# Five early slots, last routing tiles between them, and 1024-wide weight splits in a chain of attention and two expert layers

## The chip, the cores and the metric

The kernel runs on one core of one Trainium2 chip. The metric is device time in microseconds (us) for one execution of the whole program, as the median of three runs.

## What is computed

Three layers follow one another, with 4608 tokens of 512 values. The first is attention over keys and values that are pooled in groups of eight (8 batches, 8 heads, 576 queries, 72 pooled keys). The second is a gated product of two dense layers. The third sends each token to the one of eight experts that its logits choose. Cut to what matters:

```python
k_p = k.reshape(B, H, Sp, 8, D).mean(axis=3)          # v_p alike
attn = softmax(scale * q @ k_p.T)                     # 576 x 72 per head
x = (attn @ v_p), heads side by side                  # 4608 x 512
x = (x @ w_a * (x @ w_b)) @ w_out                     # 512 -> 1536 -> 512
logits = x @ w_gate                                   # 4608 x 8
e = argmax(logits); gate = softmax(logits)[e]
out = gate * (relu(x @ w1[e]) @ w2[e])                # 512 -> 1024 -> 512
```

## The kernel before

The engines are TensorE (PE, matmuls), VectorE (DVE), ScalarE (ACT), GpSimd (POOL) and SyncE (SP, which issues most DMAs). Each engine works through its own queue in order. Every f32 operand of a large matmul is split into a high part (a cast on ACT) and a low part (a subtraction, mostly on DVE), and each product is three matmuls: high x high, high x low, low x high. The order of instructions on each engine is laid out by a planner of the framework, from program order, priorities (`tc.high_priority()`) and its own model of durations. `tc.issue_after(ins)` forces the instructions of its block that run on the same engine as `ins` to stand behind `ins`.

**Start.** `half(b, j)` (L482) does the attention of one batch in two parts of 256 and 320 queries, in tiles of up to 128 queries. For each tile `softmax` (L404) makes scores on PE, their extremes on DVE (`mx`), 16 exponent steps on ACT (`pt`) and the division. For batch 0 `softmax` also builds `tails` on POOL, and `turned` (L523) transposes the probabilities on PE into `tp` and splits them into `th` and `tl`; the other batches go through DRAM instead (`send`, `receive`). Then `av` (L555) multiplies with the values. Meanwhile `convert(f)` (L620) splits the twelve pieces of the second layer's weights with ACT and DVE, `chain` forcing the first pieces behind steps of batch 0's softmax, and each stored piece releases the load of a later one (`load_raw`). `first` (L690) runs the second layer on batch 0 as its weights come in.

**Middle.** `moe1(s)` (L728) runs the second layer on tokens 512 at a time, nine times, with the attention of a later batch and the routing of an earlier result between its steps. `finish` copies four result tiles of 128 tokens (`x1s`) and makes a `route` generator for each (L640). Its first stage, up to `yield t`, computes the eight logits of a tile with eight products on DVE (L645), the winner and the exponents. Its second stage ranks the tokens with two small matmuls (`rk`, L670 and L671) and writes them with an indirect DMA from POOL into `rows` (L684), a DRAM table with one region per expert.

**Slots.** The third layer runs in slots of 256 tokens (`big`) or 128 (`small`) of one expert. A `Slot` (L190) has `load` (eight pieces of its expert's weights: DMA to `wr`, then the two parts into `w`), `fetch` (a gather of its tokens from `rows` by SP), `transpose` (L231 on DVE, then the split into `x`), `mm1` (96 matmuls of 256 columns for a big one, with `hidden` splitting each 512 columns of the relu into `hh` on ACT and `hl` on DVE), and `mm2` (48 matmuls of 512 columns for a big one, then `y` on ACT and an indirect DMA from POOL to the output). The weight tiles `w` rotate through 12 buffers, one and a half slots.

The first `NEARLY` = 4 slots are early: `early_table` fills their expert and position after the eighth of the nine steps, from the tokens known by then. The other 14 big slots and 5 small ones (some more under a condition at the end) come from `slot_table` (L906), which needs every token's rank. In the trace names end in `e` for early slots, `b` for big and `s` for small ones: `hle` is `hl` of an early slot, `gxb` the gathered rows of a later big one.

The order around the end of the middle part stands by hand, here from L886 on. The first stages of the last four routing tiles come ahead of all slots:

```python
for g in routes:
    while next(g) is None:
        pass
...
slots[1].load(0, 1, 2, 3)
slots[0].mm1()
slots[1].transpose()
...
slots[1].mm1()
with tc.issue_after(slots[1].last):
    step(routes, 99)
```

Then, in phase two (L1004), the table, and a loop over the slots that loads and transposes the next slot's input around each slot's `mm1` (L1022) and `mm2`. In the stage of the early slots the output tiles `y` come from the same pool as `x1s` (`p_x1`, L850). The weight buffers of phase two are a pool of its own (`p_wr`, 8 buffers), placed where the memory of the middle part was.

## Time and profile before

| what | value |
|---|---|
| median of 3 runs | 1544.84 us (1542.69 to 1544.87) |
| the profiled execution | 1544.62 us |
| its span, first to last instruction | 1542.8 us |
| PE busy | 1469.5 us, 95% |
| DVE, ACT, POOL busy | 984.4, 727.8, 313.3 us |
| mean granted clock of PE | 0.982 |

The profile's page gives the busy share of each engine in forty slices of the span, tenths of a slice as digits. Further views are tables of the same by chosen windows, lists of what each engine waited for, a timeline of instructions, groups of instructions by line, and the chain of waits that ended last. A matmul's duration overlaps with the next one's, so that the distance of two starts is the cost of one.

### The profile page before, as it was taken

How to read it: one execution, taken by the hardware profiler on the slowest of the kernel's cores; microseconds unless marked ns; L12 is line 12 of the kernel's file. 1: busy time of each engine (PE TensorE's matmuls, PEld its weight loads, DVE VectorE, ACT ScalarE, POOL GpSimd, SP SyncE). 2: the span in 40 equal slices, each digit the busy share in tenths (PEclk: the TensorE clock that was granted, in tenths of full speed). 3: DMA queues.
4: the chain of work that ended last, by engine and by line, in shares of the span. 5: the costliest groups of instructions: out<-in, count | busy, mean ns of one | idle time of the engine just before them, and what ended most of it. 6: DMA issues, size and time to landing. Idle time of an engine off the chain costs nothing.

```text
span 1542.8 us, 23808 instructions
## 1 busy us (share of the span) xinstructions
PE 1469.5 (95%) x7848; PEld 1255.5 (81%) x7848; DVE 984.4 (64%) x2446; ACT 727.8 (47%) x1878; POOL 313.3 (20%) x393
## 2 busy tenths in 40 slices
PE   4599899999999999999999999998989999999997
PEld 3499788888888888888888888887878898998986
DVE  8958594584664864845942727638867675757560
ACT  7858443534433433433432113234367665757561
POOL 2110112112111110210210000121233343433341
PEclk8799999999999999999999999999999999999998
DMA  8658644436435445344333224426289996969740
GB/s 308 207 195 290 202 150 129 154 117 178 137 113 164 130 127 167 116 132 151 122 123 99 76 82 164 157 76 191 102 274 319 301 297 213 289 217 294 237 144 28
DMA packets 145389, 268.97 MB, mean 174 GB/s; under 512 B 27049, under 2 KB 81065, under 8 KB 145264
## 3 DMA queue, kind: packets, MB, share of 16 engines
q1 hardware_dynamic: 139104, 247.44, 50.8%
q0 software_dynamic: 6160, 19.99, 3.3%
q8 instruction: 63, 1.03, 0.3%
q14 instruction: 62, 0.51, 0.1%
HBM read 223.45 MB, written 44.16 MB: 173 GB/s over the span
## 4 chain that ended last, share of the span: by engine, by line
PE 80%; DMA 7%; DVE 4%; ACT 4%; issue 3%; SPq 1%; POOL 1%; POOLq 0%; DVEq 0%; ACTq 0%
PE ab L754 11%; PE ab L755 11%; PE ab L756 11%; PE po L740 6%; PE po L741 6%; PE po L742 6%; PE hpb L273 3%; PE hpb L275 3%; PE hpb L274 3%; PE ypb L295 3%; PE ypb L296 3%; PE ypb L297 3%; PE sc L411 2%; PE av L555 2%; DMA wre<-in_w 1%
## 5 line engine op out<-in xcount | busy, mean ns | idle before, releaser
L755 PE MATMUL ab<-x,wab 128*128 128x512 f32 x768 | 302.3, 394 | 2.6 <-DVE x L187 2.6
L754 PE MATMUL ab<-x,wab 128*128 128x512 f32 x768 | 300.5, 394 | 0.2 <-ACT a L760 0.2
L756 PE MATMUL ab<-x,wab 128*128 128x512 f32 x768 | 300.5, 392 | 0.0
L645 DVE CUSTOM_DVE_ANT_0 junk<-x1s,wg 128x512 bf16<-128x512 f32 x288 | 205.4, 713 | 17.7 <-ACT x1s L781 11.6
L755 PEld LDWEIGHTS ab<-x,wab 128*128 128x128 f32 x768 | 144.2, 188 | 32.1 <-DVE x L187 2.8
L754 PEld LDWEIGHTS ab<-x,wab 128*128 128x128 f32 x768 | 144.2, 188 | 30.8 <-issue 1.0
L756 PEld LDWEIGHTS ab<-x,wab 128*128 128x128 f32 x768 | 144.3, 188 | 28.6 <-issue 0.2
L740 PE MATMUL po<-wo,gh 128*128 128x512 f32 x384 | 151.4, 394 | 0.0
L741 PE MATMUL po<-wo,gh 128*128 128x512 f32 x384 | 151.1, 394 | 0.0
L209 DVE TENSOR_TENSOR wb<-wrb,wb 128x512 fp32r<-128x512 f32 x168 | 126.2, 802 | 37.5 <-ACT wb L208 37.5
L742 PE MATMUL po<-wo,gl 128*128 128x512 f32 x384 | 143.5, 391 | 0.0
L208 ACT CAST wb<-wrb 128x512 fp32r<-128x512 f32 x224 | 126.0, 621 | 34.9 <-DMA wrb<-in_w 16.2
L186 ACT CAST gh<-a 128x512 fp32r<-128x512 f32 (+1 forms) x120 | 69.9, 584 | 137.1 <-DVE a L765 131.0
L760 ACT COPY a<-ab 128x512 f32<-128x512 f32 x96 | 56.8, 592 | 160.2 <-PE ab L756 123.3
L765 DVE TENSOR_TENSOR a<-ab,a 128x512 f32<-128x512 f32 x96 | 66.0, 687 | 96.9 <-PE ab L756 85.8
L684 POOL DMA_INDIRECT rows<-x1s,posu x36 | 39.0, 1083 | 434.7 <-DVE posu L683 176.9
L273 PE MATMUL hpb<-xb,wb 128*128 128x256 f32 x448 | 127.1, 284 | 0.0
L274 PE MATMUL hpb<-xb,wb 128*128 128x256 f32 x448 | 126.6, 283 | 0.0
L275 PE MATMUL hpb<-xb,wb 128*128 128x256 f32 x448 | 126.6, 283 | 0.0
L419 ACT ACTIVATE pt<-sc,mx 128x72 f32<-128x72 f32 (+1 forms) x320 | 98.5, 327 | 54.4 <-DVE mx L416 41.8
L447 POOL TENSOR_TENSOR pq<-pt,sm 128x256 f32<-128x256 f32 (+1 forms) x70 | 48.6, 713 | 341.5 <-DVE sm L425 208.5
L209 POOL TENSOR_TENSOR wb<-wrb,wb 128x512 fp32r<-128x512 f32 x56 | 76.9, 1394 | 91.5 <-ACT wb L208 90.5
(263 smaller groups left out, 3332.4 us busy)
## 6 DMA issues: line engine op xcount, KB each, us to landing
wrb<-in_w SPq DMA_DIRECT2D x112, 512.0 KB
wo<-wos SPq DMA_DIRECT2D x96, 512.0 KB
wrs<-in_w SPq DMA_DIRECT2D x40, 512.0 KB
wre<-in_w SPq DMA_DIRECT2D x32, 512.0 KB
vr<-in_v SPq DMA_DIRECT2D x48, 256.0 KB
raw<-in_wab SPq DMA_DIRECT2D x24, 512.0 KB
turns<-pq SPq DMA_DIRECT2D x28, 384.0 KB
gp<-turns SPq DMA_DIRECT2D x112, 96.0 KB
```

The source lines that it names most:

```text
L208: nc.scalar.copy(w[:, 0, hs], raw[:, hs])
L209: (nc.gpsimd if i%4==3 else nc.vector).tensor_tensor(out=w[:, 1, hs], in0=raw[:, hs], in1=w[:, 0, hs].bitcast(F32), op=ALU.subtract)
L273: nc.tensor.matmul(hp[:, fi], lhsT=wh, rhs=self.x[:, 0, k], start=k == 0, stop=False)
L274: nc.tensor.matmul(hp[:, fi], lhsT=wh, rhs=self.x[:, 1, k], start=False, stop=False)
L275: i = nc.tensor.matmul(hp[:, fi], lhsT=wl, rhs=self.x[:, 0, k], start=False, stop=k == NK - 1)
L645: nc.vector.tensor_tensor_reduce(out=junk, in0=x1s[:, :DM], in1=wg[:, e, :], scale=1.0, scalar=0.0, op0=ALU.mult, op1=ALU.add, accum_out=l ...
L740: nc.tensor.matmul(po[t], lhsT=gh[:, ts_], rhs=w[:, 0], start=f == 0, stop=False)
L741: nc.tensor.matmul(po[t], lhsT=gh[:, ts_], rhs=w[:, 1], start=False, stop=False)
L742: nc.tensor.matmul(po[t], lhsT=gl[:, ts_], rhs=w[:, 0], start=False, stop=f == NF1 - 1)
L754: nc.tensor.matmul(o, lhsT=wh, rhs=xh, start=k == 0, stop=False)
L755: nc.tensor.matmul(o, lhsT=wh, rhs=xl, start=False, stop=False)
L756: nc.tensor.matmul(o, lhsT=wl, rhs=xh, start=False, stop=k == NK - 1)
```

## The change

- `NEARLY` goes from 4 to 5, so there are 5 early slots and 13 later big ones; the three small tiles of each turn of `early_table` share a buffer.
- In `Slot.load` each piece of 1024 columns is cast by one instruction on ACT and subtracted by one on DVE, instead of two of 512 each with the subtraction on POOL for pieces 3 and 7.
- `hidden` keeps its DVE instruction as `self.hid`.
- For batch 0 the building of `tails` moves from `softmax` into `turned`, and a tile's `turned` is called after the next tile's `softmax`.
- The output tiles of the early stage get a pool of their own, `p_y`, with two buffers.
- The first stages of the four last routing tiles (`rate`) are called one by one after `slots[0].mm1()`, `slots[0].mm2()`, `slots[1].mm1()` and `slots[1].mm2()`; their second stages (`rank`) two by two after `slots[1].mm1()` and `slots[2].mm1()`. Loads, transposes and fetches around them are set anew; `slots[4].fetch()` comes ahead of `slots[1].mm2()`.
- In phase two the loop starts at slot 2, and the transpose of the first late slot stands behind `s.hid`, the last hidden part of the last early slot.

```diff
-NEARLY = 4
+NEARLY = 5
...
-                for h in range(2):
-                    hs = slice(h * n // 2, (h + 1) * n // 2)
-                    nc.scalar.copy(w[:, 0, hs], raw[:, hs])
-                    (nc.gpsimd if i%4==3 else nc.vector).tensor_tensor(
-                        out=w[:, 1, hs], in0=raw[:, hs], in1=w[:, 0, hs].bitcast(F32), op=ALU.subtract
-                    )
+                nc.scalar.copy(w[:, 0], raw)
+                nc.vector.tensor_tensor(out=w[:, 1], in0=raw, in1=w[:, 0].bitcast(F32), op=ALU.subtract)
...
-                (send if by_dma else turned)(o, m, pf)
-                if len(sent) > 1:
-                    yield
-                    receive()
+                if by_dma:
+                    send(o, m, pf)
+                    if len(sent) > 1:
+                        yield
+                        receive()
+                else:
+                    sent.append((o, m, pf))
+                    if len(sent) > 1:
+                        turned(*sent.pop(0))
...
-        p_x1 = p2["p_y"] = ph1.enter_context(tc.tile_pool(name="p_x1", bufs=4))
+        p_x1 = ph1.enter_context(tc.tile_pool(name="p_x1", bufs=4))
...
+                right("p_y", 2)
...
-        for g in routes:
-            while next(g) is None:
-                pass
...
+        last4 = list(routes)
+
+        def rate():
+            g = last4.pop(0)
+            while next(g) is None:
+                pass
+
+        def rank(n, ins):
+            with tc.issue_after(ins):
+                for _ in range(n):
+                    for _ in routes.pop(0):
+                        pass
+
         slots[1].load(0, 1, 2, 3)
         slots[0].mm1()
+        rate()
         slots[1].transpose()
         slots[1].load(4, 5, 6, 7)
         slots[2].fetch()
         slots[3].fetch()
+        slots[0].mm2()
+        rate()
         slots[2].load(0, 1, 2, 3)
-        slots[0].mm2()
+        slots[1].mm1()
+        rank(2, slots[1].last)
+        rate()
+        slots[2].transpose()
         slots[2].load(4, 5, 6, 7)
-        slots[1].mm1()
-        with tc.issue_after(slots[1].last):
-            step(routes, 99)
+        slots[4].fetch()
+        slots[1].mm2()
+        rate()
+        slots[3].load(0, 1, 2, 3)
+        slots[2].mm1()
+        rank(2, slots[2].last)
         wra.close()
...
             if nx:
-                nx.transpose()
-                if i > 1:
-                    nx.load(4, 5, 6, 7)
+                with tc.issue_after(s.hid) if i + 1 == NEARLY else nullcontext():
+                    nx.transpose()
+                nx.load(4, 5, 6, 7)
```

## Rows read from the trace of the kernel before

**Rows 1.** The page: busy tenths of PE in 40 equal slices of the span.

```profile
PE   4599899999999999999999999998989999999997
```

**Rows 2.** Windows of 5 us: length, busy time (count) of PE, PEld, DVE, ACT, POOL; clock; DMA.

```profile
1070.00:1075.00 5.00, 0.00 (x0) 0.00 (x0) 5.00 (x16) 1.02 (x3) 0.00 (x0) 0.84 0.31 105
1075.00:1080.00 5.00, 4.83 (x22) 4.83 (x23) 5.00 (x14) 0.00 (x0) 0.00 (x0) 0.50 0.00 2
...
1125.00:1130.00 5.00, 0.47 (x4) 0.27 (x3) 0.28 (x1) 0.00 (x0) 0.98 (x1) 0.81 0.93 202
1130.00:1135.00 5.00, 3.41 (x16) 3.41 (x17) 4.89 (x8) 3.76 (x7) 0.00 (x0) 0.51 0.98 388
```

**Rows 3.** Waits, after 1040 us: who waited for whom, us, times, longest.

```profile
PE hpe L273 <- DVE hle L241: 5.3, 1, 5.3
...
PE ype L295 <- ACT ye L299: 1.4, 1, 1.4
...
ACT ye L299 <- DMA rows<-x1s,posu: 7.5, 3, 3.6
...
PE hpe L273 <- DVE hle L241: 6.1, 1, 6.1
...
PE yps L297 <- DVE hls L241: 0.9, 1, 0.9
```

**Rows 4.** Timeline 1062 to 1075: start, duration, engine, line, tiles; waits in brackets.

```profile
1062.56 6.90 POOL L209 TENSOR_TENSOR we<-wre,we 128x512 fp32r<-128x512 f32 x4 [19.24 <-ACT we L208]
...
1066.53 0.60 ACT L240 ACTIVATE hhe<-hpe 128x512 fp32r<-128x512 f32 x1 [0.21 <-PE hpe L275]
...
1068.23 1.78 DVE L645 CUSTOM_DVE_ANT_0 junk<-x1s,wg 128x512 bf16<-128x512 f32 x1
...
1073.08 0.68 DVE L645 CUSTOM_DVE_ANT_0 junk<-x1s,wg 128x512 bf16<-128x512 f32 x1
...
1074.43 0.68 DVE L241 SCALAR_TENSOR_TENSOR hle<-hpe,hhe 128x512 fp32r<-128x512 f32 x1
```

**Rows 5.** Timeline of DVE, 1124 to 1131.

```profile
1124.03 0.18 DVE L1002 TENSOR_TENSOR slot_b<-bb_f,ee_f 128x22 int32<-128x22 f32 x1
1129.72 1.24 DVE L231 STREAM_TRANSPOSE xtb<-gxb 128x1024 f32<-128x1024 f32 x1 [5.50 <-DMA gxb<-rows]
1130.88 0.65 DVE L241 SCALAR_TENSOR_TENSOR hle<-hpe,hhe 128x512 fp32r<-128x512 f32 x1
```

**Rows 6.** Groups by line and shape, 14 to 120 us: busy us, mean ns.

```profile
L603 DVE TENSOR_TENSOR wab<-raw,wab 128x1024 fp32r<-128x1024 f32 x5 | 6.2, 1240 | 0.0
...
L602 ACT CAST wab<-raw 128x1024 fp32r<-128x1024 f32 x5 | 5.8, 1165 | 0.7 <-DVE raw L599 0.7
```

**Rows 7.** Groups by line and shape, POOL, 1200 to 1480 us.

```profile
L209 POOL TENSOR_TENSOR wb<-wrb,wb 128x512 fp32r<-128x512 f32 x40 | 54.6, 1384 | 64.0 <-ACT wb L208 63.1 <-issue 0.8
```

**Rows 8.** One window, from the end of the middle part (columns as in rows 2).

```profile
1042.40:1155.00 112.60, 99.31 (x610) 88.90 (x610) 87.80 (x256) 51.09 (x96) 33.07 (x31) 0.94 0.61 187
```

**Rows 9.** Groups by line and shape, DVE, 1042.4 to 1131.6 us.

```profile
L645 DVE CUSTOM_DVE_ANT_0 junk<-x1s,wg 128x512 bf16<-128x512 f32 x32 | 25.1, 785 | 2.3 <-ACT x1s L781 2.3
```

**Rows 10.** Timeline of PE in the last slot: starts of successive matmuls.

```profile
1521.40 0.28 PE L275 MATMUL hpb<-xb,wb 128*128 128x256 f32 x1
1521.52 0.39 PE L295 MATMUL ypb<-wb,hhb 128*128 128x512 f32 x1
1521.75 0.40 PE L296 MATMUL ypb<-wb,hhb 128*128 128x512 f32 x1
```

**Rows 11.** Timeline of the start, 24 to 32 us.

```profile
24.87 1.09 PE L527 MATMUL tp<-ident,pt 128*128 128x128 f32 x4 [5.92 <-DVE pt L429]
...
31.05 0.58 PE L555 MATMUL av<-th,vx 128*128 128x256 f32 x1 [3.44 <-DVE th L496]
...
31.76 0.69 ACT L602 CAST wo_s<-rawo 128x512 fp32r<-128x512 f32 x1 [1.92 <-DVE rawo L599]
```

**Rows 12.** The chain of waits, 0 to 100 us: start, us, what.

```profile
21.08 2.42 ACT pt L419 x16
```

More of the change, by code (lines that the diff above doesn't have):

```diff
@@ L159, in early_table @@
         for s in range(NEARLY):
-            g = pool.tile([P, E], F32, name=f"g_e{s}")
-            se = pool.tile([P, 1], F32, name=f"se_e{s}")
+            g = pool.tile([P, E], F32, tag="g_e", name=f"g_e{s}")
+            se = pool.tile([P, 1], F32, tag="se_e", name=f"se_e{s}")
             nc.vector.tensor_scalar(out=g, in0=end, scalar1=float(s), scalar2=None, op0=ALU.is_le)
@@ L166, in early_table @@
             nc.vector.tensor_tensor(out=g, in0=g, in1=fe, op=ALU.mult)
-            sj = pool.tile([P, 1], F32, name=f"sj_e{s}")
+            sj = pool.tile([P, 1], F32, tag="sj_e", name=f"sj_e{s}")
             nc.vector.tensor_reduce(out=sj, in_=g, axis=AX.X, op=ALU.add)
@@ L240, in hidden @@
                 nc.scalar.activation(self.hh[:, fs], src, AF.Relu)
-                nc.vector.scalar_tensor_tensor(
+                i = nc.vector.scalar_tensor_tensor(
                     out=self.hl[:, fs], in0=src, scalar=0.0, in1=self.hh[:, fs].bitcast(F32),
@@ L244, in hidden @@
                 )
+                self.hid = i.ins
         def mm1(self):
@@ L433, in softmax @@
                     chain.append((ex.ins, nm.ins))
-                tails = p_at.tile([P, 2, 4, TB], F32, tag="pq", name=f"tails{name}", bufs=1)
-                for g in range(2):
-                    nc.gpsimd.tensor_copy(
-                        tails[:n, g, 0].rearrange("q (p i s) -> q p i s", p=2, i=2),
-                        bass.AP(pt.tensor, pt.offset + g * 4 * SP, [p0, (2 * SP, 2), (2 * SP - TAIL, 2), (1, TAIL)]),
-                    )
-                nc.gpsimd.tensor_copy(tails[:n, :, 1:], tails[:n, :, 0:1].to_broadcast([n, 2, 3, TB]))
-                tf = tails.rearrange("q g i c -> q (g i c)")
-                return [pt[:n, c * 2 * SP + TAIL:c * 2 * SP + TAIL + P] for c in range(4)] + [
-                    tf[:n, g * P:(g + 1) * P] for g in range(2)
-                ]
+                return pt[:n]
             pq = p_at.tile([P, 4, NB6, TB], F32, tag="pq", name=f"pq{name}", bufs=1)
@@ L521, in receive, with turned @@
                 cut(0, NB6, o, m, xt[:, :w].rearrange("q j k b -> q k j b"), TB)
-            def turned(o, m, pf):
+            def turned(o, n, pt):
+                p0 = (pt.ap[0][0], n)
+                tails = p_at.tile([P, 2, 4, TB], F32, tag="pq", name=f"tails{b}_{j}_{o}", bufs=1)
+                for g in range(2):
+                    nc.gpsimd.tensor_copy(
+                        tails[:n, g, 0].rearrange("q (p i s) -> q p i s", p=2, i=2),
+                        bass.AP(pt.tensor, pt.offset + g * 4 * SP, [p0, (2 * SP, 2), (2 * SP - TAIL, 2), (1, TAIL)]),
+                    )
+                nc.gpsimd.tensor_copy(tails[:n, :, 1:], tails[:n, :, 0:1].to_broadcast([n, 2, 3, TB]))
+                tf = tails.rearrange("q g i c -> q (g i c)")
+                pf = [pt[:n, c * 2 * SP + TAIL:c * 2 * SP + TAIL + P] for c in range(4)] + [
+                    tf[:n, g * P:(g + 1) * P] for g in range(2)
+                ]
+                m = n
                 for c0, c1 in ((0, 4), (4, NB6)):
@@ L547, in half @@
             while sent:
-                receive()
+                receive() if by_dma else turned(*sent.pop(0))
                 yield
@@ L1010, in moe_chain_kernel @@
         for i, s in enumerate(slots):
-            if i == 0:
+            if i < 2:
                 continue
             nx = slots[i + 1] if i + 1 < len(slots) else None
-            if i + 2 < len(slots) and i + 2 > NEARLY:
+            if NEARLY < i + 2 < len(slots):
                 slots[i + 2].fetch()
-            if nx:
-                if i > 1:
+            if i > 2:
+                if nx:
                     nx.load(0, 1, 2, 3)
-            if i + 2 == NEARLY:
-                slots[NEARLY].fetch()
-            if i > 1:
+                if i + 2 == NEARLY:
+                    slots[NEARLY].fetch()
                 s.mm1()
             if nx:
-                nx.transpose()
-                if i > 1:
-                    nx.load(4, 5, 6, 7)
+                with tc.issue_after(s.hid) if i + 1 == NEARLY else nullcontext():
+                    nx.transpose()
+                nx.load(4, 5, 6, 7)
             s.turn(1)
```

## The prediction

> **What bounds the kernel now.** I read the page's forty slices first. TensorE (PE) is at 9 in nearly all of them [rows 1], so a change counts only where PE stands still or is held at its low clock. That leaves three places: the first three slices, the two low slices after 1041 us where the first product ends and the early slots begin, and the last slice. Then come the 5 us windows of the second place: PE does nothing from 1070 to 1075 and next to nothing from 1125 to 1130, and in the window behind each hole the granted clock is 0.50 and 0.51, the lower of its two levels (1.2 of 2.4 GHz) [rows 2]. PE's list of waits gives the holes names: 5.3 us in the first matmuls of a slot for `hle`, 6.1 us for `hle` again, 1.4 us for `ye`, and 0.9 us near the end for `hls` [rows 3]. A matmul that runs at half clock loses half its time: 4.83 x 0.5 = 2.4 us behind the first hole and 3.41 x 0.5 = 1.7 us behind the second [rows 2]. So the first hole costs 7.7 us, the second 7.8, the others 2.3: 17.8 us in all is what the middle and the tail of the kernel can return.
>
> **Why PE stands still.** First hole: the ScalarE half of the hidden tile was begun at 1066.53, yet VectorE (DVE) came to its half only at 1074.43, nearly 8 us later [rows 4]. DVE was not waiting, it was behind: from 1062.56 GpSimd (POOL) worked four weight halves for 6.90 us, and the routing's products next to it took 1.78 us where one alone takes 0.68 [rows 4]. Second hole: it is order. DVE finished the slot table at 1124.03, and its next instruction was the transpose of the first late slot's rows; it stood 5.50 us for the gather to land, and `hle`, ready behind it, ran at 1130.88 [rows 5]. The `ye` wait is a buffer: ScalarE waited 7.5 us in three pieces for `rows<-x1s,posu`, since in this stage the outputs take their tiles from the pool of the routing's rows [rows 3].
>
> **The change, part by part.**
>
> *Weight halves on ACT and DVE, 1024 wide.* The 1024-wide forms already stand in the trace: 1.17 us for the cast on ACT and 1.24 us for the subtraction on DVE [rows 6]. A piece costs DVE 1.24 us instead of two halves of about 0.7; a slot's pieces 3 and 7 come over from POOL, where a half takes 1.38 us [rows 7]. In the stretch 1042 to 1155 DVE is busy 87.8 of 112.6 us [rows 8]. About eight pieces move to it there, 8 x 1.24 = 9.9 us, and the contention goes: 1.78 - 0.68 = 1.1 us for each slowed operation [rows 4], of which the same view has some seven, 7 to 8 us. DVE's total is then about 90 us and hardly moves, but the lateness in bursts goes. In the many slots after that PE is full [rows 1], so there the edit is worth nothing but the 0.9 us at the end, where the late `hls` also stood behind subtractions next to POOL. If that cover were gone, every DVE delay would show.
>
> What POOL's neighbour costs is also told by the Trainium skill (SBUF — State Buffer, Who interferes with whom): a VectorE instruction with two SBUF inputs and a GpSimd instruction that reads SBUF exclude one another for a whole instruction. The trace agrees in kind, 1.78 us against 0.68 [rows 4]. By that rule up to all 6.90 us of POOL's stretch would come back to DVE and no rest of the first hole would be left, which makes the sum below 2.5 us lower, 1526.5 us.
>
> *Routing of the last four tiles spread out.* Its 32 products are 25.1 us of DVE [rows 9] and all of them now lie ahead of the first slot's matmuls in program order. After it, eight lie behind `slots[0].mm1()`, eight behind `slots[0].mm2()`, eight behind `slots[1].mm1()`, eight behind `slots[1].mm2()`. A matmul of 256 columns starts every 0.12 us and one of 512 every 0.23 [rows 10], so `mm1` is 96 x 0.12 = 11.5 us and `mm2` 48 x 0.233 = 11.2 us. Adding each phase's weights (4 x 1.24), hidden halves, transposes and eight products (6.3 us and some small operations), DVE is asked for 14, 12, 16 and 14 us in these four phases of 11.3: about 10 us behind at the end, and level again three phases later. The backlog falls on routing and table, not on `hle`, which has priority, but it can reach it. First hole: between 0 left and all 7.7 left; I take 2.5 left, since its cause (POOL) is gone and its load is not: 5.2 us gained.
>
> *A fifth early slot, and the late slot's transpose behind the last `hle`.* The table now has to be ready for slot 5 instead of 4, while the last routing starts one slot later, so the distance from routing to first late slot stays at five phases, 56 us. What changes is the order: the transpose can't stand ahead of any `hle` of slot 4 (`issue_after(s.hid)`), and behind it lie `mm2`'s 11.2 us, which need nothing of it. That covers a wait of 5.50 us twice. The second hole's 7.8 us go. What is late next: the second weight half of `e3` is the first load out of phase two's pool, whose memory is free only when the last routing's rows have landed, and it is needed one phase after that; also `e4`'s fetch reads `rows` behind two of the last writes, and on SP `e3`'s first weights queue behind it, which is covered, since they wait for `e1`'s weights to come free anyway and are needed some 25 us later. New stall: 0 at best, 6.1 us at worst (today's hole in a new place); I take 1.5, near zero, because a whole phase lies between. Gain 7.8 - 1.5 = 6.3.
>
> *Own output pool.* `ye` no longer waits for the rows: 1.4 us.
>
> *One more early slot in the early table* is one more turn of eight small DVE operations, while PE is full and DVE mostly idle: nothing. The number of slots, weights and matmuls is the same.
>
> *Scores ahead of transposes in the first batch.* PE now does the first tile's transposes before the second tile's scores, and so waits 5.92 us for the second tile's `pt` at 24.87 and 3.44 us before `av` at 31.05 [rows 11]. After it the second scores come as soon as the first are done. But ACT and DVE are nearly full there: the second tile's 16 exponent steps, 2.42 us on the chain [rows 12], then go ahead of weight conversions that also gate PE. ACT's own idle time is small, 1.92 us ahead of 31.76 [rows 11]. From +2.4 (conversions pushed back, nothing gained) to -5.9 (the whole `pt` wait); I take -2, the size of ACT's idle time that can be filled, and all that follows moves along.
>
> **The sum.** The profiled execution took 1544.62 us (span 1542.8), 0.2 under the median of 1544.84, so no correction. 1544.6 - 5.2 - 6.3 - 1.4 - 0.9 - 2.0 = 1528.8, say 1529 us.
>
> **Rivals.**
>
> *DVE stays the bound of the early slots.* Everything of POOL is now on it, and 90 us of work in about 102 us leaves little. For it: DVE is busy 5.00 of 5 us in both windows from 1070 to 1080 [rows 2]. Against: part of that was the backlog that POOL's neighbourhood had left. Then the first hole stays and a hole opens at `e3`; left are half the second hole, `ye`, the tail and the start: 1544.6 - 3.9 - 1.4 - 0.9 - 2 = 1536 (1533 to 1540). Chance 0.18.
>
> *The start loses.* The exponents push the first conversions: +2.4 instead of -2.0, 1533. Chance 0.10.
>
> *The start gives the whole wait* and no hole is left: 1544.6 - 7.7 - 7.8 - 1.4 - 0.9 - 5.9 = 1521. Chance 0.10.
>
> *Wide casts break the full stage: slower.* PE fills a hidden tile in 24 x 0.12 = 2.9 us and has two; ACT (0.60) and DVE (0.68) must have read the older one by then [rows 4]. With one wide cast and one wide subtraction just begun ahead of them the time is 1.17 + 1.24 + 1.28 = 3.7 us, 0.8 too long; with halves it fits. There are 18 x 4 = 72 such tiles. All late would cost 58 us; from one in three (19 us) the gain is eaten and the kernel is slower, about 1548 to 1555. Against it: operations next to POOL are as long today and PE doesn't wait there, and matmuls of the slot before are mixed in. Chance 0.07.
>
> *The change does not do what it says:* instructions are laid out by a planner, and the new program order may put the products and the transpose where they were. Then only `ye` and the tail remain: 1542. Chance 0.07.
>
> **How the numbers follow.** Forecast 0.48, its own range 1523 to 1534. About 0.2% (3 us) is what a measurement here can tell from no change. Faster: forecast, first three rivals: 0.86; the last rival is split evenly at the border of 1541.5, so faster 0.88, within 0.2% 0.05, slower 0.07. The range takes in the forecast, the start either way and DVE as the bound: 1520 to 1540.
>
> **What would show it.** Right: no 5 us window below 4 of PE between 1045 and 1155, clock 1.00 throughout; `hle` within 2 us of its ACT half; the transpose of `gxb` behind the last `hle` of `e4`; no L209 on POOL; first `av` about 29. Wrong: PE waiting for `hle` or for `we` of `e3` in the middle, or waits for `hhb` and `hlb` scattered over 1200 to 1480, or `av` no earlier than 31.

## The result, and the profile after

| what | before | after |
|---|---|---|
| median, runs side by side | 1544.58 us (4 runs) | 1528.3 us (1526.77 to 1530.03, 4 runs) |
| ratio | | 0.9898 [0.9883, 0.9914] |
| the profiled execution, its span | 1544.62, 1542.8 us | 1530.03, 1528.0 us |
| PE, DVE, ACT, POOL busy | 1469.5, 984.4, 727.8, 313.3 us | 1467.8, 990.4, 709.6, 185.8 us |
| mean granted clock of PE | 0.982 | 0.988 |

The change saves 15.8 us (13.3 to 18.1 by the interval); 1529 was forecast. The sum hit in good part by luck: two of its large terms were wrong, and they cancelled. The stretches show it first; they are read from one execution of each kernel, and that of the changed kernel is the longest of its four. The span is cut at the first 512-column matmul of `moe1`, behind the last matmul of the middle part, and behind the last matmul of all. Columns are as in [rows 2]. Before:

```profile
0.00:182.80 182.80, 138.72 (x890) 125.47 (x890) 135.15 (x245) 126.00 (x363) 25.79 (x66) 0.91 0.69 239
182.80:1042.60 859.80, 856.80 (x3977) 703.75 (x3977) 521.93 (x1615) 317.32 (x991) 120.97 (x190) 1.00 0.42 132
1042.60:1531.80 489.20, 473.93 (x2985) 426.28 (x2983) 327.32 (x588) 283.86 (x526) 165.56 (x136) 0.99 0.72 229
1531.80:1542.80 11.00, 0.00 (x0) 0.00 (x0) 0.00 (x0) 0.64 (x1) 0.98 (x1) 0.61 0.07 26
```

After:

```profile
0.00:172.70 172.70, 137.96 (x890) 124.39 (x890) 133.73 (x246) 124.22 (x363) 29.04 (x66) 0.95 0.74 253
172.70:1035.30 862.60, 859.80 (x3987) 705.72 (x3986) 521.02 (x1615) 315.85 (x980) 106.94 (x184) 1.00 0.42 131
1035.30:1517.20 481.90, 469.99 (x2975) 423.06 (x2973) 335.66 (x502) 269.08 (x354) 48.80 (x50) 0.99 0.72 232
1517.20:1528.00 10.80, 0.00 (x0) 0.00 (x0) 0.00 (x0) 0.49 (x1) 0.98 (x1) 0.63 0.07 25
```

The first number behind the range is its length. The start is 10.1 us shorter with the same 890 matmuls, where 2 were forecast. The slots are 7.3 us shorter, where 5.2 + 6.3 + 1.4 + 0.9 = 13.8 were forecast. The middle is 2.8 us longer; about 1 us of that is ten matmuls of the first slot that now lie ahead of the cut (3987 against 3977). The other 1.8 us are within what this stretch differs by from kernel to kernel: over all traces of this document it takes 857.4 to 860.6 us in the five kernels without these ten matmuls, and 858.4 to 862.4 in the nine with them. Together -10.1 + 2.8 - 7.3 - 0.2 = -14.8, the difference of the two spans.

**The start.** Of PE's timeline, one set of transposes and the first `av` of each part of batch 0 (start, duration, engine, line; in brackets the idle time before and who ended it):

```profile
16.14 1.08 PE L527 MATMUL tp<-ident,pt 128*128 128x128 f32 x4 [4.19 <-DVE sm L421]
...
25.06 0.58 PE L560 MATMUL av<-th,vx 128*128 128x256 f32 x1 [4.50 <-DVE th L483]
...
56.94 0.69 PE L527 MATMUL tp<-ident,pt 64*128 64x64 f32 x4 [3.52 <-DVE pt L426]
...
65.66 0.63 PE L560 MATMUL av<-th,vx 128*128 128x320 f32 x1 [3.69 <-DVE th L483]
```

The first `av` is at 25.06 instead of 31.05 [rows 11], 6.0 us earlier. The second, for the 320 queries, is 11.5 us earlier: before, it stood at 77.17. The same shows in every trace: the first 512-column matmul of `moe1` comes between 171.6 and 174.6 us in the ten kernels with the new start, and between 182.9 and 184.9 in the three with the old one (180.0 where only its first part is new).

**The early slots.** Windows of 5 us, the only ones between 1045 and 1170 that fall below 4 of PE, and the one behind them:

```profile
1060.00:1065.00 5.00, 3.33 (x24) 2.81 (x24) 5.00 (x15) 2.07 (x3) 0.61 (x1) 1.00 0.51 163
...
1105.00:1110.00 5.00, 3.99 (x34) 3.78 (x32) 4.05 (x27) 1.09 (x2) 1.11 (x2) 1.00 0.14 54
1110.00:1115.00 5.00, 3.56 (x27) 3.23 (x27) 3.06 (x9) 2.68 (x5) 0.85 (x1) 1.00 0.85 292
...
1155.00:1160.00 5.00, 3.85 (x33) 3.65 (x31) 1.86 (x3) 0.24 (x2) 0.98 (x1) 1.00 0.93 306
1160.00:1165.00 5.00, 2.25 (x6) 1.86 (x7) 3.99 (x4) 4.44 (x6) 0.00 (x0) 0.65 1.00 374
1165.00:1170.00 5.00, 5.00 (x28) 4.86 (x27) 3.17 (x5) 2.32 (x4) 0.00 (x0) 0.66 1.06 361
```

PE's waits between 1030 and 1180 (us, times, longest):

```profile
PE hpe L270 <- DVE hle L237: 4.3, 3, 2.4
PE ypb L292 <- ACT hhb L236: 3.9, 1, 3.9
PE ype L292 <- ACT hhe L236: 1.3, 2, 1.0
```

Both holes of [rows 2] are closed. What is left of the first is 1.67 us at 1063, and the granted clock stays at 1.00. The wait for `ye` of [rows 3] is gone. But a new hole stands where no window of before was low, at 1158 to 1163. It costs 3.9 us of waiting, and the clock is 0.65 and 0.66 around it: 5.00 x 0.34 = 1.7 us in the window behind, and up to 2.25 x 0.35 = 0.8 us in its own. These 6.4 us are most of why the slots give 7.3 and not 13.8: a new stall of 1.5 is already in the 13.8, so the hole explains 4.9 of the missing 6.5. The rest is among smaller waits, as those of 2.45 us at 1111 and 1.03 at 1135.

Its cause is read backwards. PE waits for ACT's half of the first late slot's hidden tile:

```profile
1162.75 0.80 PE L292 MATMUL ypb<-wb,hhb 128*128 128x512 f32 x1 [3.90 <-ACT hhb L236]
```

ACT has that `hhb` in its queue behind a cast of the next slot's weights, and stands 4.76 us there for the load:

```profile
1154.41 0.71 ACT L186 CAST xs<-xts 128x256 fp32r<-128x256 f32 x2 [0.86 <-DVE xts L227]
1159.89 1.04 ACT L206 CAST ws<-wrs 128x1024 fp32r<-128x1024 f32 x1 [4.76 <-DMA wrs<-in_w]
1161.16 1.04 ACT L206 CAST ws<-wrs 128x1024 fp32r<-128x1024 f32 x1 [0.23 <-DMA wrs<-in_w]
1162.11 0.59 ACT L236 ACTIVATE hhb<-hpb 128x512 fp32r<-128x512 f32 x1
```

SP issued these loads (`wrs`) only at 1155.20, behind the fetch of the second late slot, and no DMA at all between 1141.4 (1132.17 + 9.23) and 1152.47:

```profile
1132.17 9.23 SPq L204 DMA_DIRECT2D wrb<-in_w  x8
1152.47 1.89 SPq L216 DMA_DIRECT2D gxb<-rows  x4
1154.56 0.40 SPq L221 DMA_DIRECT2D endsb<-rows  x1
1155.20 4.77 SPq L204 DMA_DIRECT2D wrs<-in_w  x8
```

That fetch needs a buffer that the first late slot's transpose has to free, and that is the transpose which the change ties behind the last `hle` of `e4`. On DVE it stands right behind it:

```profile
1148.34 0.68 DVE L237 SCALAR_TENSOR_TENSOR hle<-hpe,hhe 128x512 fp32r<-128x512 f32 x1
1148.94 1.24 DVE L227 STREAM_TRANSPOSE xtb<-gxb 128x1024 f32<-128x1024 f32 x1
```

So the theory after the result was: the start is worth some 10 us, since the same wait stood in it several times; POOL is the first hole; the second hole is closed by the time that a fifth slot gives; and the tie makes the new hole.

### The profile page after: what moved, and what is told of

Same layout as the page of the kernel before. It is cut to its first block, busy times and chain, and to the rows that moved or that the text cites. A ratio compares the mean times of both kernels' runs of the same rounds, so it can differ in the third digit from the quotient of the medians.

```text
span 1528.0 us, 23427 instructions
## 1 busy us (share of the span) xinstructions
PE 1467.8 (96%) x7848; PEld 1253.2 (82%) x7848; DVE 990.4 (65%) x2362; ACT 709.6 (46%) x1694; POOL 185.8 (12%) x301
## 3 DMA queue, kind: packets, MB, share of 16 engines
q8 instruction: 63, 1.03, 0.3%
## 5 line engine op out<-in xcount | busy, mean ns | idle before, releaser
L650 DVE CUSTOM_DVE_ANT_0 junk<-x1s,wg 128x512 bf16<-128x512 f32 x288 | 199.8, 694 | 17.6 <-ACT x1s L786 12.9
L207 DVE TENSOR_TENSOR wb<-wrb,wb 128x1024 fp32r<-128x1024 f32 x104 | 124.7, 1220 | 39.0 <-ACT wb L206 34.8
L206 ACT CAST wb<-wrb 128x1024 fp32r<-128x1024 f32 x104 | 107.2, 1047 | 31.9 <-PE ypb L294 12.6
L270 PE MATMUL hpb<-xb,wb 128*128 128x256 f32 x416 | 119.0, 286 | 0.5 <-DVE hlb L237 0.5
L271 PE MATMUL hpb<-xb,wb 128*128 128x256 f32 x416 | 118.4, 285 | 0.0
L272 PE MATMUL hpb<-xb,wb 128*128 128x256 f32 x416 | 118.3, 284 | 0.0
L187 DVE TENSOR_TENSOR gl<-a,gh 128x512 fp32r<-128x512 f32 (+1 forms) x120 | 76.1, 634 | 18.4 <-ACT gh L186 18.2
```

Source lines behind the costliest of these rows:

```text
L206: nc.scalar.copy(w[:, 0], raw)
L207: nc.vector.tensor_tensor(out=w[:, 1], in0=raw, in1=w[:, 0].bitcast(F32), op=ALU.subtract)
L270: nc.tensor.matmul(hp[:, fi], lhsT=wh, rhs=self.x[:, 0, k], start=k == 0, stop=False)
L271: nc.tensor.matmul(hp[:, fi], lhsT=wh, rhs=self.x[:, 1, k], start=False, stop=False)
L272: i = nc.tensor.matmul(hp[:, fi], lhsT=wl, rhs=self.x[:, 0, k], start=False, stop=k == NK - 1)
L650: nc.vector.tensor_tensor_reduce(out=junk, in0=x1s[:, :DM], in1=wg[:, e, :], scale=1.0, scalar=0.0, op0=ALU.mult, op1=ALU.add, accum_out=l ...
```

## The experiments

Gains are given against the kernel before, run beside each.

### The start alone, and its first part alone

`start_only` is the kernel before with the reordering of batch 0 and nothing else:

```diff
-                (send if by_dma else turned)(o, m, pf)
...
+                else:
+                    sent.append((o, m, pf))
+                    if len(sent) > 1:
+                        turned(*sent.pop(0))
...
```

> The kernel before with only the start changed: for batch 0 a tile's transposes are called behind the next tile's softmax, and the tails are built there. Theory A (the start is worth far more than forecast): the trace of the changed kernel reaches its first 512-column matmul 10 us earlier, and nothing else of the change touches that stretch, so this kernel gains 7 to 10 us and takes 1535 to 1538 us; the first value product of batch 0 begins at about 25 us, the second set at about 66. Theory B (the forecast): the start is worth 2 us, 1543 us, and the rest of the 10 us came from elsewhere.

Measured: 1535.68 us, ratio 0.9936 [0.9914, 0.9959], a gain of 9.9 us (6.3 to 13.3). `start_j0` undoes it for the second part, the 320 queries:

```diff
-                    if len(sent) > 1:
+                    if len(sent) > 1 or j:
                         turned(*sent.pop(0))
```

> As start_only, but in the second part of batch 0 (320 queries) each tile's transposes follow its own scores at once, as before; only the first part (two tiles) is changed. Theory A1 (the gain is carried by the first part, all behind it moves along): the same time as start_only within 1 us. Theory A2 (both parts give their share: 6 us at the first value products, 5 more at the second): about 4 to 5 us slower than start_only, near 1540 us, with the first value product at 25 us and the second set at about 71.

Measured: 1542.38 us, ratio 0.9981 [0.9967, 0.9995], a gain of 2.9 us (0.8 to 5.1). So some 7 of the 9.9 us come from the second part. (Both kernels have the `tails` in `turned`; what that move does by itself was not tried.) The row which says so had been in the kernel before all along. PE's waits in its first 183 us, the first line alone:

```profile
PE tp L527 <- DVE pt L429: 17.7, 4, 5.9
```

This wait stood there four times, 17.7 us in all, and the forecast priced the one of 5.92 [rows 11]. In `start_j0` PE's wait in the second part is back, and even joined into one, and its second `av` is late again:

```profile
70.75 0.66 PE L530 MATMUL tp<-ident,pt 64*128 64x64 f32 x4 [9.06 <-DVE pt L429]
...
72.78 0.63 PE L563 MATMUL av<-th,vx 128*128 128x320 f32 x1 [0.73 <-DVE th L486]
```

In `start_only` that `av` starts at 65.34, 7.4 us earlier. The clock belongs to it: in the changed kernel the stretch up to `moe1` has a mean of 0.95 instead of 0.91.

### The weight pieces alone, and the change without them

`split_only` is the kernel before with the 1024-wide pieces on ACT and DVE; `halves` is the changed kernel with the old ones. The edit, forward in the one and backward in the other:

```diff
-                for h in range(2):
-                    hs = slice(h * n // 2, (h + 1) * n // 2)
-                    nc.scalar.copy(w[:, 0, hs], raw[:, hs])
-                    (nc.gpsimd if i%4==3 else nc.vector).tensor_tensor(
...
+                nc.scalar.copy(w[:, 0], raw)
+                nc.vector.tensor_tensor(out=w[:, 1], in0=raw, in1=w[:, 0].bitcast(F32), op=ALU.subtract)
```

> The kernel before with only the weight splits changed to 1024 columns on ACT and DVE, nothing on POOL. Theory A (POOL next to DVE is what made DVE late): the first hole of 5.3 us shrinks to 0 to 2.5 us and the half clock behind it goes, the second hole and the wait for ye stay; with the late wait near the end gone the gain is 5 to 8 us, 1537 to 1540 us. Theory B (DVE is simply full there, its total does not change): no difference, 1544 to 1545, or slower by up to 2 us.

Measured: 1540.43 us, ratio 0.9974 [0.9958, 0.9991], a gain of 4.0 us (1.4 to 6.5), less than the 5 to 8 expected. PE waits 1.33 us in place of the first hole, with the clock at 1.00; the second hole stays in another form, 3.69 us for a weight piece of ACT and a clock of 0.56 behind it. The wait for `hls` near the end is gone, but in the late slots PE waits four times for `hhb`, 1.6 us in all.

> The changed kernel with the weight halves as before: two casts and two subtractions of 512 columns per piece, those of pieces 3 and 7 on POOL. Theory A (POOL next to DVE was part of the first hole): products beside POOL take 1.78 us again, a wait for hle of 3 us or more returns between 1060 and 1112, 3 to 7 us are lost, 1531 to 1535 us. Theory B (spreading the routing alone is enough, and DVE is relieved by POOL): 1526 to 1530 us, waits for hle at most 4.3 us in all as in the changed kernel.

Measured: 1536.25 us, ratio 0.9958 [0.9947, 0.9969]: the gain falls from 15.8 to 6.5 us, so inside the changed kernel the edit is worth some 9 us, more than the 3 to 7 expected. The first hole is back, in its old size and with the low clock behind it. But it is not all of the 9 us: two more holes follow, 6.13 us at 1119.84 for a weight piece of ACT, which had stood 10.07 us ahead of `ye`, and the new hole, now of 5.27 us, at 1172.75, each with windows at clock 0.50. From the start of the middle's last matmul to the end of the last matmul, the slots of `halves` take 490.6 us, against 489.5 before and 481.9 in the changed kernel: in this trace nothing is left of what the slots gave. PE's wait at the first hole and the windows:

```profile
1066.59 0.58 PE L274 MATMUL hpe<-xe,we 128*128 128x256 f32 x1 [5.55 <-DVE hle L241]
```

```profile
1060.00:1065.00 5.00, 1.04 (x6) 0.53 (x4) 5.00 (x10) 1.62 (x3) 2.12 (x2) 0.89 0.46 160
1065.00:1070.00 5.00, 3.41 (x16) 3.41 (x17) 5.00 (x15) 0.00 (x0) 0.00 (x0) 0.50 0.03 9
```

And DVE's products of the routing beside POOL's two pairs of halves, of 3.44 us from 1053.34 and 2.55 us from 1058.32:

```profile
1053.82 1.80 DVE L654 CUSTOM_DVE_ANT_0 junk<-x1s,wg 128x512 bf16<-128x512 f32 x1
...
1057.99 3.43 DVE L654 CUSTOM_DVE_ANT_0 junk<-x1s,wg 128x512 bf16<-128x512 f32 x1
...
1064.51 0.68 DVE L654 CUSTOM_DVE_ANT_0 junk<-x1s,wg 128x512 bf16<-128x512 f32 x1
...
1065.86 0.68 DVE L241 SCALAR_TENSOR_TENSOR hle<-hpe,hhe 128x512 fp32r<-128x512 f32 x1
```

The same product takes 1.80 and 3.43 us beside POOL and 0.68 alone, and the `hle` for which PE waits comes at 1065.86. These two products alone take 1.12 + 2.75 = 3.9 us longer. The routing is spread in this kernel and the hole is there all the same; in `split_only` it is not spread, and PE waits only 1.33 us at that place. So the old pieces made the first hole, not the place of the products. The edit also makes the pieces wide, and no run takes POOL out without that; that it is POOL is read from the slowed operations, which in this stretch stand only beside its halves and are gone with them. The Trainium skill (SBUF — State Buffer, Who interferes with whom) says of such a pair that one blocks the other for a whole instruction. The trace agrees in kind: the product of 3.43 us is about as long as POOL's pair of 2.55 and its own 0.68.

### What closed the second hole

`no_hid` takes the tie out of the changed kernel:

```diff
-                with tc.issue_after(s.hid) if i + 1 == NEARLY else nullcontext():
-                    nx.transpose()
+                nx.transpose()
```

> The changed kernel without the tie that puts the first late slot's transpose behind the last hidden part of the last early slot. Theory A (the tie is what closed the second hole of the kernel before): DVE takes the transpose ahead of an hle of e4 and waits there for the gather, PE stops for hle for 3 to 6 us near 1130 to 1140 and its clock falls, 3 to 8 us are lost, 1531 to 1536 us. Theory B (with a fifth early slot the gather has landed by then anyway, and the tie only holds back the fetch behind it): no new wait for hle, the buffer of the gathered rows comes free earlier, the wait of 3.90 us for hhb near 1162 goes, 1523 to 1527 us.

Measured: 1525.91 us, ratio 0.9884 [0.986, 0.9908]. The gain is 17.9 us (14.2 to 21.6), not told apart from the 15.8 of the changed kernel, and not smaller. The transpose is back ahead of the last `hle`, and the gather has nearly landed:

```profile
1128.98 1.25 DVE L227 STREAM_TRANSPOSE xtb<-gxb 128x1024 f32<-128x1024 f32 x1 [1.50 <-DMA gxb<-rows]
```

1.50 us instead of 5.50 [rows 5]. So the tie is not what shortened this wait. The order counts all the same: without the tie the transpose of the small slot, too, stands ahead of an `hle` of `e4` and waits for its gather, and PE stops, with a lower clock behind it (DVE, PE, and the window):

```profile
1138.16 0.71 DVE L227 STREAM_TRANSPOSE xts<-gxs 128x512 f32<-128x512 f32 x1 [1.46 <-DMA gxs<-rows]
1138.80 0.65 DVE L237 SCALAR_TENSOR_TENSOR hle<-hpe,hhe 128x512 fp32r<-128x512 f32 x1
```

```profile
1139.51 0.39 PE L270 MATMUL hpe<-xe,we 128*128 128x256 f32 x1 [2.31 <-DVE hle L237]
```

```profile
1140.00:1145.00 5.00, 5.00 (x28) 4.77 (x27) 4.66 (x5) 3.97 (x6) 1.80 (x1) 0.66 1.03 412
```

That is 2.31 + 5.00 x 0.34 = 4.0 us, which theory B had not expected. `fifth_only` is the kernel before with a fifth early slot and nothing more (the three shared small tiles go with it, for the memory):

```diff
-NEARLY = 4
+NEARLY = 5
...
-            if i + 2 < len(slots) and i + 2 > NEARLY:
+            if i + 2 < len(slots) and (i + 2 > NEARLY or i == 2):
```

> The kernel before with a fifth early slot and nothing else of the change: no spread routing, no tie of the transpose, no own output pool, weight halves of 512 with POOL, the old start. The forecast put the whole second hole (7.8 us) to the order of DVE's queue and gave the credit to the tie behind the last hidden part; the changed kernel without the tie, however, showed no such hole. Theory A (the fifth slot alone gives the gather its time): DVE no longer stands 5 us before the late slot's transpose ahead of an hle, the hole near 1125 goes or shrinks to under 3 us, the first hole of 7.7 us stays, 1536 to 1541 us. Theory B (the lateness of DVE and ACT decides, and the table is only drawn later): a hole of like size stays, for the gather or for weights, 1543 to 1548 us.

Measured: 1539.13 us, ratio 0.9957 [0.9942, 0.9972], a gain of 6.6 us (4.3 to 9.0). Its first hole stays (5.36 us for `hle`). DVE's first late transpose waits for nothing now, but `hle` is late in this kernel from another cause, four subtractions next to POOL that take 6.26 us:

```profile
1128.82 6.26 DVE L209 TENSOR_TENSOR we<-wre,we 128x512 fp32r<-128x512 f32 x4 [2.23 <-ACT we L208]
1135.01 0.68 DVE L241 SCALAR_TENSOR_TENSOR hle<-hpe,hhe 128x512 fp32r<-128x512 f32 x1
...
1142.88 1.24 DVE L231 STREAM_TRANSPOSE xtb<-gxb 128x1024 f32<-128x1024 f32 x1
```

The fifth slot alone removes the wait for the gather, but in this trace not what PE loses there: PE's waits from 1120 to 1140 are 0.41 + 0.69 + 1.43 + 0.84 + 2.00 = 5.4 us. In the windows from 1130 and 1135 PE is busy 2.01 and 4.26 us at clock 0.74 and 0.57, which costs 2.01 x 0.26 + 4.26 x 0.43 = 2.4 us more. Together that is as much as the second hole's 7.8. (This profiled execution, of 1544.95 us, was the longest of the kernel's six; where the other five gain their 5 to 9 us it does not show.)

Nor is the fifth slot alone in shortening the wait for the gather. `split_only` has four early slots and no tie, and there it is

```profile
1125.43 1.25 DVE L227 STREAM_TRANSPOSE xtb<-gxb 128x1024 f32<-128x1024 f32 x1 [1.31 <-DMA gxb<-rows]
```

while PE waits 3.69 us for the weight piece. So either edit takes most of the 5.50 us away, and with either alone PE loses about as much to another wait at that place. The hole is closed only in kernels that have both, and with them the rest of the change: with the tie, or, but for the 4.0 us above, without it. No run has the two edits alone.

### What makes the new hole

`no_hid` already shows that the tie makes it: without the tie SP issues the fetch of the second late slot some 9 us earlier, and PE is busy 5.00 of 5 us at clock 1.00 in both windows from 1155 to 1165.

```profile
1143.23 2.78 SPq L216 DMA_DIRECT2D gxb<-rows  x4
```

`fetch_late` keeps the tie and cuts the chain behind it. It is the changed kernel with the fetch of the second late slot moved behind the small slot's first weight loads, so that these no longer stand behind it on SP:

```diff
-            if NEARLY < i + 2 < len(slots):
+            if NEARLY < i + 2 < len(slots) and i != NEARLY:
                 slots[i + 2].fetch()
...
+                if i == NEARLY:
+                    slots[i + 2].fetch()
                 s.mm1()
```

> The changed kernel with one line moved: in the turn of the first late slot, the fetch of the second late big slot (gxb) comes behind the load of the small slot's first four weight pieces instead of ahead of it. SP issues in order; in the changed kernel that fetch waits on SP until 1152.47 for its buffer, the weight loads wrs stand behind it until 1155.20, ACT then waits 4.76 us for wrs at 1159.89 ahead of hhb, and PE waits 3.90 us at 1162.75 and runs at clock 0.65 around it. Theory A (the new hole comes from what is queued behind the fetch on SP): wrs is issued before 1150, the wait of 3.9 us for hhb and the clock of 0.65 behind it go, 3 to 6 us are gained, 1522 to 1525.5 us. Theory B (the loads wait for their own buffers, or the gather that now comes later is missed by its transpose): the hole stays or turns up one slot later, 1527 to 1530 us.

Measured: 1523.05 us (1521.67 to 1523.93), ratio 0.9871 [0.9852, 0.989], a gain of 19.9 us (17.0 to 22.8), about 4 more than the change. Its interval overlaps with that of the changed kernel by a little, its runs don't (1526.77 was the shortest there), and the trace shows the hole gone. Windows of `fetch_late`:

```profile
1155.00:1160.00 5.00, 4.67 (x36) 4.17 (x35) 5.00 (x8) 3.37 (x7) 1.50 (x2) 1.00 1.01 333
1160.00:1165.00 5.00, 5.00 (x35) 4.59 (x35) 4.81 (x6) 2.97 (x4) 0.00 (x0) 1.00 1.04 316
```

The clock is 1.00, and ACT's first casts of `ws` now run from 1150.96 without a wait. Theory A holds. By its runs this is faster than both kernels; two further edits on top of it were tried.

`keep_y`: in the changed kernel ACT stood 6.95 us ahead of `ye` at 1108.91, with an `hhe` behind it, and PE waited 2.45 us at 1111.44 for the `hle` that follows. Here the slot `e2` goes on using the early output pool (phase two's is named `p_y2`):

```diff
...
+            if i == 2:
+                p2["p_y"] = p2["p_y2"]
...
```

> The changed kernel with the fetch of the second late slot moved behind the small slot's first weights (as in fetch_late, 1523.05 us) and one edit more: the third early slot (e2) still writes its outputs to the early stage's own pool, and phase two's pool of four is used from the fourth slot on. In the changed kernel ACT stands 6.95 us before the ye at 1108.91, until the last write of rows issued at 1105.69 has landed, with hhe of e3 behind it at 1110.06, and PE waits 2.45 us for hle at 1111.44. Theory A (phase two's output buffers lie on the memory of the routing's tiles, so the first ye that uses them waits for the last write): that wait of ACT goes, the wait of PE for hle near 1111 goes too, 1.5 to 4 us are gained against fetch_late, 1519 to 1521.5 us. Theory B (DVE's slot table and the late second weight half of e3 hold hle there anyway): 1522 to 1524 us.

Measured: 1524.97 us, ratio 0.9859 [0.9828, 0.989]. ACT's wait is gone (`ye` runs at 1101.28 and 1102.73), so it had been the memory under phase two's pool. But PE's time is not: its wait for `hle` near 1110 is still 1.03 us, and waits of 0.3 and 0.5 us for `we` come at 1113 and 1114. The gain is not told apart from that of `fetch_late`: nearer to theory B for the time.

`keep_y_tie4`: `e4`'s transpose tied as the change ties the next one, since in `fetch_late` it stood 6.61 us for its gather ahead of an `hle`, for which PE waited 2.20 us.

```diff
-                with tc.issue_after(s.hid) if i + 1 == NEARLY else nullcontext():
+                with tc.issue_after(s.hid) if NEARLY - 1 <= i + 1 <= NEARLY else nullcontext():
```

> The kernel keep_y with the transpose of the last early slot (e4) tied behind the last hidden part of e3, as the changed kernel ties that of the first late slot. In fetch_late DVE takes e4's transpose at 1094.70 after 6.61 us of waiting for its gather, ahead of an hle of e2 for which PE then stands 2.20 us. Theory A (any gather's transpose in DVE's queue ahead of an hle costs PE): the 2.2 us go and nothing else comes, 1517 to 1520 us. Theory B (held back, it keeps its buffer longer, the fetch of the first late slot and all loads queued behind it on SP come later, and ACT then waits for weights): 1521 to 1526 us.

Measured: 1525.88 us, ratio 0.9863 [0.9836, 0.9891], no gain over `keep_y`. In `keep_y` the 2.20 us had already shrunk to 0.50, and with the tie a wait of 0.43 for `hhe` stands in its place; and PE now waits 3.8 us once for another `hhe`, with the clock at 0.57 between 1135 and 1140. The tie bought nothing and a new wait came.

### The spread routing, and the output pool

`no_spread` is the changed kernel with the first stages of the four last tiles ahead of all slots again, and their second stages together:

```diff
+        for _ in range(4):
+            rate()
         slots[1].load(0, 1, 2, 3)
         slots[0].mm1()
-        rate()
...
-        rank(2, slots[1].last)
+        rank(4, slots[1].last)
```

> The changed kernel, but the first stages of the four last routing tiles come ahead of all slots and all four second stages behind the second slot's first matmuls, as in the kernel before; five early slots, the splits and the rest stay. Theory A (spreading takes the products out of the first phases and so keeps DVE ahead of PE): 3 to 5 us slower than the changed kernel, 1531 to 1534 us, with PE waiting for hle in the second slot. Theory B (with POOL gone there is room enough, and what the fifth slot gives is cover): no difference, 1527 to 1530, or a little faster, since the table and the first late gather are ready one phase earlier.

Measured: 1531.21 us, ratio 0.9902 [0.9874, 0.993]. By the ratio the spread is worth 0.7 us, by the medians 2.9; it can't be told from nothing. The trace has another set of holes, the largest of 5.46 us at 1104.76 for the first weights of `e3`: on SP these loads stand behind `e4`'s fetch, which waits here until 1096.63 for the writes of `rows`, and in the changed kernel until 1089.13.

`old_y` gives the early outputs back to the pool of the routing's rows, the routing still spread:

```diff
-        p_x1 = ph1.enter_context(tc.tile_pool(name="p_x1", bufs=4))
+        p_x1 = p2["p_y"] = ph1.enter_context(tc.tile_pool(name="p_x1", bufs=4))
...
-                right("p_y", 2)
```

> The changed kernel with the early slots' outputs again in the pool of the routing's rows. Theory A (the pool was the 1.4 us wait for ye): ACT waits for the writes of rows ahead of ye again, PE waits 1 to 3 us for ye, and in the in-order queue of ACT casts and hidden halves stand behind, 1 to 5 us lost, 1529.5 to 1533 us. Theory B (with the routing spread the tiles come free in time): no wait of PE for ye, 1527 to 1529.5 us.

Measured: 1540.55 us, ratio 0.9979 [0.997, 0.9989]: only 3.2 of the 15.8 us are left, so here the pool is worth some 12 us, more than any theory had. ACT, in order, stands ahead of `ye` for the routing's writes, and `ye`, or an `hhe` behind it, is late for PE (3.3 us at 1081, 3.4 at 1127). The longest wait for `hhe`, 4.5 us at 1099, stands behind casts that wait for their loads, and was not traced further. The profiled execution, of 1545.8 us, is the longest of ten. ACT's waits between 1030 and 1180, and PE's:

```profile
ACT ye L296 <- DMA rows<-x1s,posu: 13.2, 2, 8.2
```

```profile
PE ype L292 <- ACT hhe L236: 7.9, 2, 4.5
PE ype L292 <- ACT ye L296: 3.3, 1, 3.3
...
PE hpe L270 <- DVE hle L237: 2.5, 1, 2.5
PE rk L675 <- DVE x1s L680: 2.0, 1, 2.0
```

`nospread_old_y` undoes both:

> The changed kernel with the first stages of the last four routing tiles ahead of all slots again, and with the early outputs in the routing's pool again: both edits undone together. Undone alone, the first cost about 3 us (1531.21) and the second about 12 (1540.55). Theory A (the output pool matters so much only because the spread routing keeps its tiles longer, past the first slots' outputs): both undone cost 3 to 6 us, 1531 to 1535 us. Theory B (the output pool is worth 12 us by itself): 1541 to 1545 us.

Measured: 1536.02 us, ratio 0.9937 [0.9913, 0.9962], a gain of 9.7 us (5.9 to 13.4). Without the spread the pool is worth 15.1 - 9.7 = 5.4 us, with it 15.8 - 3.2 = 12.6: the two edits belong together, as theory A had it. Whether the pool counts by itself is not shown: the intervals of 15.1 (10.8 to 19.5) and 9.7 overlap. With the old pool the spread loses (9.7 without it, 3.2 with it).

## Why the prediction was right, and where it was not

The time was right: 1529 forecast, 1528.3 measured. That was luck in good part, since the start gave some 8 us more than forecast and the slots 6.5 less. By its own steps:

**First hole: right, in cause and size.** 2.5 us were to be left, 1.67 are, and without the clock's loss. Taking the pieces off POOL did it (`halves` brings back 5.55 us), and DVE's total hardly moves, as forecast: 90.78 of 112.60 us from 1035.3, against 87.80 [rows 8] and a forecast of 90. The lone product is back at 0.68 us; the 32 of them take 21.8 us instead of 25.1 [rows 9]. These 3.3 us are three slowed products; with five other operations of DVE that were slowed to between 1.2 and 1.7 us in the same stretch, contention gave back about 8 us, as the prediction had it (7 to 8). From the rule of the Trainium skill (SBUF — State Buffer, Who interferes with whom) the prediction had worked out that no rest would be left. The trace doesn't bear that inference out, and does not speak against the rule: no operation of DVE is slowed there any more, and the 1.67 us at 1063 come from a subtraction of 1.22 and a product of 0.69 us on DVE ahead of `hle`. The step "spread out" had no part in it that could be measured.

**Second hole: gone as forecast, but credited to the wrong edit.** The prediction said that the fifth slot leaves the distance as it was and that the order alone does it. `no_hid` has the old order, and the wait of 5.50 us is 1.50; `fifth_only` has only the slot, and it is gone; `split_only` has only the wide pieces, and it is 1.31. In neither of the two last is PE's loss gone; it is gone only where both edits are, with the rest of the change. The order was right in kind and mis-sized: in `no_hid` the small slot's transpose ahead of an `hle` costs 4.0 us, where the prediction gave all 7.8 to the order.

**The new stall: mis-sized, 1.5 us against 6.4, and elsewhere.** It was sought at `e3`'s second weights. There is little there: 2.45 us at 1111 and 1.03 at 1135. The step that failed is the one which costed the tied transpose at nothing because `mm2` needs nothing of it. What was not followed is the buffer that this transpose reads: it came free later, the next fetch stood on SP for it, the loads `wrs` stood behind the fetch, ACT stood for them, and `hhb` behind that. Each of the four queues is worked in order; the wait went through all of them. `no_hid`, without the tie, has no such hole, and `fetch_late` cuts the chain at one link.

**`ye` and the pool: right for the kernel before, but not independent.** 1.4 us was the wait of [rows 3]. Together with the spread the old pool would have cost 12.6 us. Since the change did both, the sum did not show it.

**The tail: 0.9 us were returned, and given back.** The wait for `hls` is gone. (It is gone in `halves` too, where POOL is back; so what took it away is not shown.) But in the full stage PE now waits 1.6 us in four pieces for `hhb` and 0.5 us in three for `hlb`, where before it was 0.5 for `hhb`. Every kernel with the wide pieces has those 1.6 us for `hhb`, and `halves` has no wait of PE there at all. So the rival of the wide casts exists in kind, at about 1.6 us of its 58.

**The start: wrong, 2 us against 9.9 (6.3 to 13.3), outside of its bounds (+2.4 to -5.9).** The mechanism was right, the term mis-sized: the bound was the one wait of 5.92 us in the first part, while the edit acts on both parts. For the first part alone the 2 us were about right (`start_j0`, 2.9). The list of waits had it four times with 17.7 us. The fear that the exponents would hold up the weight conversions was empty: the stretch is shorter with the same busy time of PE.

**The rivals.** DVE did not stay the bound, and the change did what it says: no subtraction on POOL is left, and the late transpose stands behind the last `hle`. The list of what would show it was too strict in one point, since three windows between 1045 and 1155 are below 4 (3.33, 3.99 and 3.56), and wrong in another: the first `av` came at 25, not 29. In the chances, an even split of the last rival's 0.07 gives 0.895 for faster and 0.035 for within 0.2%; 0.88 and 0.05 don't follow from it.

**Sums of parts.** Alone, the start gives 9.9, the fifth slot 6.6 and the pieces 4.0 us: 20.5 together, against 15.8; with intervals of 2 to 4 us on each this alone is not a clear difference. Taken out, the pieces cost 9, more than twice of what they give alone, and the pool 12.6. No such number is a property of the edit; it depends on which wait ends last once the others are gone.

What stays open: what in the fifth slot gives the 6.6 us of its median, what the order is worth once the tie's new hole is removed, and whether the spread is worth the 0.7 to 2.9 us that its two readings give.

## What to carry to other kernels

When an edit removes a wait, look in the list of waits for every place where the same wait stands, not only for the one on the timeline you opened. When an instruction is tied to a later place, follow the buffer that it frees: whoever needs this buffer, what is queued behind that on its engine, and what stands behind those. And test edits by taking each out of the final kernel as well as by adding it alone, since for the weight pieces here the two differ by a factor of two.

## What the runs showed of the hardware that was not expected

A product of DVE that alone takes 0.68 us took 3.43 us beside POOL's halves (in `halves`), five times as long; the 1.78 us of [rows 4] were not the worst case. And the clock made a short wait dear: the new hole of 3.9 us carried the granted clock down to 0.65 and 0.66 in two windows, some 2.5 us more, while the waits of 1.67 and 2.45 us in the same kernel left it at 1.00. The length of the wait alone doesn't tell: in `no_hid` one of 2.31 us had 0.66 in the window behind it.
